# Two attentions in one kernel: Pool's tables, tile 1's low parts and the fourth group's fetches in another order at the start

## The chip, the cores and the metric

One core of a Trainium2 chip. The metric is the time on the device of one execution, in microseconds (us). Five engines work side by side, each in the order of its own queue: TensorE (PE; its weight loads are shown as PEld), VectorE (DVE), ScalarE (ACT), GpSimd (POOL, here Pool) and SyncE (SP), which does nothing here but issue DMAs. An instruction waits until what it needs is done, and everything behind it in its queue waits with it. A DMA that an engine issues goes through the same queue; the transfer then runs by itself and reports when it has landed.

## The reference

`x` is 2048 x 576. Two attentions of 32 heads with 18 features each run over it, and a gate per row mixes them. A has keys and values of its own for each head, B one key and one value for all heads; B's queries and keys are larger, so that its softmax needs true row maxima.

```python
x = A_x                                      # [1, 2048, 576]
g = _sigmoid((x * gate_w).sum(-1, keepdims=True))
# a: q, k, v = split(x @ wqkv), 32 heads of 18
#    o = softmax(q k^T * 18**-0.5) v, then o @ wo
a = _A_ref(x, A_wqkv, A_wo)
# b: q = x @ wq (32 heads), k = x @ wk and v = x @ wv shared by all heads
#    o = softmax(q k^T * 18**-0.5) v, then o @ wo
b = _B_ref(x, B_wq, B_wk, B_wv, B_wo)
return g * a + (1 - g) * b
```

## The kernel before, in words

All float32 work is done in pairs: a number is split into a high part (`h`, rounded to the format that TensorE multiplies fast) and a low part (`l`, the rest), and a product is made of h*h, l*h and h*l. The 64 heads ("units" u, 32 of B and then 32 of A) run one after the other: scores of keys times queries (L752), exponentials on ACT (L760), sums with the values (L767); for each of them the row maxima are taken ahead, 22 key steps early, on VectorE (L707, L716).

**The start.** Before the first scores, `x` is loaded in chunks of 256 columns (c = 0 to 7) into staging tiles (`xs`, `xsh`) and split: `high_x` on ACT, `low_x` on VectorE (L404), and `last_x` (L408), a subtraction on half the partitions, on VectorE or Pool by the chunk. `project` multiplies it with the weights of tile 0 (which holds B's key, the gate, B's value and the first queries) and tile 1, 512 columns at a time. The four stretches of 512 columns are called the first to the fourth group. Each of tile 0 leaves its bank through `leave_first`: `high` on ACT (L283), `low` on VectorE (L287), stores to the DRAM tensor `kq_d` by SP, a copy `pst` on ACT. For odd groups the differences of keys (`pd`, `pdhl`) are stored too, to `kd_d` or `ke_d`. Tile 1 leaves through `leave`, and its store is kept in the list `store`.

Keys and queries then come back from DRAM, three rows per feature: `first_back` (keys' differences `kdb`, the first group of `ksb`, query columns 0 to 1023 of `qs[0]`), `rows_back` (query columns 1024 to 1535 and 1536 to 2047, the third group of `ksb`, and `keb`, the differences of the third and fourth group), `keys_back` (queries of units 1 and 2, the rest of `ksb`, rows of ones). All of these are issued by SP, in that order. `load_w(2, ...)`, the deferred stores of `REST_ROWS` and `store` and the rows of ones are issued by Pool (L472 to L477). Two copies of one number on Pool, `seen` (L471, L474), make Pool wait for a landing first: the first for `qs[0]`, the second for `keb`.

**The lead stage** (`lead_steps`, L1162 to L1166) follows an order written out as a string. A and B are halves of a product of the projection of tiles 1 and 2 ("units" of `lead_units`: each leaves its two banks through ACT into `lst` and `pst2`, two buffers each, and is added, cast, subtracted and stored by Pool). x and y make a row maximum by way of differences: x multiplies queries by `kdb` or `keb` (the columns of the second half of a pair of groups minus those of the first), ACT takes the positive part into `xd` (L1130, four buffers); y multiplies the same queries by `ksb`, and one VectorE instruction (L1136) adds the two and takes the maximum into the table `mx` (its line names `junk` and `mx`). x comes one pair ahead of y: "x1, x2 y1, x3 y2, ...". A runs on one half of TensorE's rows beside B on the other, and x beside y. Seven banks of PSUM go round between A, B, x and y. The products are numbered in this text by their x: 1 to 16 multiply the 16 column steps of `qs[0]` (128 columns each) by `kdb`, 17 to 32 the same steps by `keb`, 33 on belong to `qs[1]`.

The tables `mx` (five, set to -3e38) and `ms` (two, set to 0) and a rounded copy of the identity, `ident_r`, are made by Pool (L499 to L505), behind all of the above in its queue. `mx` must be set before the first maximum writes into it.

Of the kernel before, what the change touches and what calls it, by code (L numbers as in the profile page):

```python
# [8 lines left out]
F32 = mybir.dt.float32  # L9
# [3 lines left out]
OP = mybir.AluOpType  # L13
# [4 lines left out]
S = 2048  # L18
# [138 lines left out]
def gated_mix_kernel(ctx: ExitStack, tc: tile.TileContext, xT, wall, wv, wo, out):  # L157
    nc = tc.nc
    P = 128

    def dma(o, i, eng=None):
        o, i = (x.bitcast(F32) if x.dtype == F32R else x for x in (o, i))
        return (eng or nc.sync).dma_start(o, i)  # L163
# [22 lines left out]
    ident = fixed.tile([P, P], F32, name="ident")  # L186
    make_identity(nc, ident)
    ident_r = fixed.tile([P, P], F32R, name="ident_r")
    qs = [fixed.tile([P, S], F32R, name=f"qs{i}") for i in range(3)]
# [20 lines left out]
    def in_turn(which):  # L210
        return bank_tile(clk.turn(which))
# [52 lines left out]
    def project(mt, c, w, parts=1):  # L264


        fp = in_turn("g")
        g = 512 // parts
        for i in range(parts):
            products(fp, w, c * 512, g * i, g)  # L270
        return fp

    def products(fp, w, x0, p0, g, n0=0, n1=len(PROJ)):

        for n, (a, b, k, kr) in list(enumerate(PROJ))[n0:n1]:
            nc.tensor.matmul(fp[:, p0:p0 + g], w[a][:kr, k, :], X[b][:kr, k, x0 + p0:x0 + p0 + g],
                             start=(n == 0), stop=(n == len(PROJ) - 1))
# [11 lines left out]
    def leave(mt, c, fp, hl=None):  # L289
        hl = hl or high(fp)  # L290
        low(fp, hl)
        return lambda: dma(qk_d[:, mt * P:(mt + 1) * P, c * 512:(c + 1) * 512].rearrange("a p f -> p a f"), hl, nc.gpsimd)

    def leave_first(c, fp):
        cs = slice(c * 512, (c + 1) * 512)
        hl = high(fp)
        to, q = kq_d[54:216, cs].rearrange("(p a) f -> p a f", a=3), hl[QR]
        tk = kq_d[0:54, cs].rearrange("(p a) f -> p a f", a=3)
        if c % 2:
            d = stp.tile([P, 512], F32, name="pd", bufs=1)  # L300
            dhl = stp.tile([P, 2, 512], F32R, name="pdhl", bufs=1)
            nc.vector.tensor_tensor(d[KR], fp[KR], KD[c - 1][KR], op=OP.subtract)
            nc.scalar.activation(dhl[KR, 0, :], d[KR], AF.Copy)
        low(fp, hl)
        dma(to[:, 1:3], q)
        dma(to[:, 0], q[:, 0])
        if c % 2:
            nc.vector.tensor_tensor(dhl[KR, 1, :], d[KR], dhl[KR, 0, :].bitcast(F32), op=OP.subtract)
            td = kd_d[KR] if c == 1 else ke_d
            dma(td[:, 0:2, :], dhl[KR])  # L310
            dma(td[:, 2, :], dhl[KR, 0])
        else:
            dma(tk[:, 0:2], hl[KR])
            dma(tk[:, 2], hl[KR, 0])
        yield
        st = KD[c] = stp.tile([P, 512], F32, name="pst", bufs=4)
        nc.scalar.activation(st, fp, AF.Copy)

        def rest():
            if c % 2:  # L320
                dma(tk[:, 0:2], hl[KR], nc.gpsimd)
                dma(tk[:, 2], hl[KR, 0], nc.gpsimd)
            dma(z_d[cs], st[ROW_G:ROW_G + 1, :], nc.gpsimd)
            dma(qk_d[:, REST, cs].rearrange("a p f -> p a f"), hl[REST], nc.gpsimd)
        REST_ROWS.append(rest)
# [8 lines left out]
    def run(gen):  # L334
        for _ in gen:
            pass
# [5 lines left out]
    def back2(t, i, x0, x1):  # L342
        for b in (SB, MB):
            back(t, i, b, x0, x1)
# [4 lines left out]
        back2(qs[0], 1, 0, 1024)  # L349

    def rows_back():
        back2(qs[0], 1, 1024, 1536)
        back2(qs[0], 1, 1536, S)
        back(ksb, 0, SB, 1024, 1536)
        dma(keb[MB:MB + 54, :], ke_d.rearrange("p a f -> (p a) f"))

    def keys_back():
        back2(qs[1], 2, 0, S)
# [10 lines left out]
    with tc.tile_pool(name="xs", bufs=1, side="right") as xsp:  # L369
        XS = []  # L370

        def load_x(c, rest=None, main=None):
            half = c < 2
            XS.append(xsp.tile([P, NKT, 256 if half else 512], F32, name="xsh" if half else "xs", bufs=2 if half else 3))
            load5(XS[c], xT[:, 256 * c:256 * c + 256] if half else xT[:, 512 * (c - 1):512 * c], rest, main)

        def main_w(st):

            w = {y: wpool.tile([P, NKT, P], F32R, name=f"w{y}", bufs=3) for y in "hl"}
            nc.scalar.activation(w["h"][:, 0:4], st[:, 0:4], AF.Copy)  # L380
            nc.vector.tensor_tensor(w["l"][:, 0:4], st[:, 0:4], w["h"][:, 0:4].bitcast(F32), op=OP.subtract)
            return w

        def last_w(st, w):
            nc.scalar.activation(w["h"][:, 4], st[:, 4], AF.Copy)
            nc.vector.tensor_tensor(w["l"][:, 4], st[:, 4], w["h"][:, 4].bitcast(F32), op=OP.subtract)

        def chunk_of(c):
            return XS[c // 2 + 1][:, :, 256 * (c % 2):256 * (c % 2) + 256] if c > 1 else XS[c]

        def high_x(c):
            nc.scalar.activation(X["h"][:, :, c * 256:(c + 1) * 256], chunk_of(c), AF.Copy)

        def rest_x(c):
            low_x(c, chunk_of(c))
            last_x(c, chunk_of(c))

        def split_x(c):
            high_x(c)
            rest_x(c)  # L400

        def low_x(c, xs):
            cs = slice(c * 256, (c + 1) * 256)
            nc.vector.tensor_tensor(X["l"][:, :, cs], xs[:, 0:4], X["h"][:, 0:4, cs].bitcast(F32), op=OP.subtract)  # L404

        def last_x(c, xs):
            xh = X["h"][64:128, 4, c * 256:(c + 1) * 256]
            (nc.gpsimd if c in (2, 4, 5, 6) else nc.vector).tensor_tensor(xh, xs[64:128, 4], xh.bitcast(F32), op=OP.subtract)  # L408

        W = [load_w(0, nc.scalar)]  # L410
        load_x(0)
        W.append(load_w(1, nc.gpsimd))
        load_x(1, nc.gpsimd)
        nc.scalar.activation(ones, ones, AF.Copy)

        warm = in_turn("m")

        def idle(n):
            for i in range(n):
                nc.tensor.matmul(warm[:, 0:304], ident, vb.rearrange("p k d -> p (k d)"), start=True, stop=True)  # L420

        idle(6)
        for c in range(2, 5):
            load_x(c)

        x0, xh = XS[0], X["h"][:, :, 0:256]
        ST = [W.pop(0) for _ in range(2)]
        WP = [main_w(ST[0])]
        nc.scalar.activation(xh[:, 0:2], x0[:, 0:2], AF.Copy)
        nc.vector.tensor_copy(xh[:, 2:4], x0[:, 2:4])  # L430
        low_x(0, x0)
        last_w(ST[0], WP[0])
        nc.scalar.activation(xh[:, 4], x0[:, 4], AF.Copy)
        last_x(0, x0)
        WP.append(prep_w(ST[1]))
        split_x(1)

        F = [in_turn("g") for _ in range(2)]
        for x in (0, 256):
            for mt in range(2):  # L440
                products(F[mt], WP[mt], 0, x, 256)
        idle(2)
        rows = leave_first(0, F[0])
        next(rows)
        split_x(2)
        split_x(3)
        run(rows)
        REST_ROWS.pop()()
        F0 = project(0, 1, WP[0], 2)
        hl = high(F[1])  # L450
        high_x(4)
        rows = leave_first(1, F0)
        next(rows)
        first_back()
        run(rows)
        store = [leave(1, 0, F[1], hl)]
        rest_x(4)
        split_x(5)
        F1 = project(1, 1, WP[1])
        split_x(6)  # L460
        split_x(7)
        F0 = project(0, 2, WP[0], 2)
        store.append(leave(1, 1, F1))
        run(leave_first(2, F0))
        F0 = project(0, 3, WP[0], 2)
        run(leave_first(3, F0))

    xdp = ph1.enter_context(tc.tile_pool(name="xdp", bufs=1, side="right"))
    keb = xdp.tile([P, 512], F32R, name="keb")
    seen = xdp.tile([P, 2], F32, name="seen")  # L470
    nc.gpsimd.tensor_copy(seen[MB:MB + 1, 0:1], qs[0][MB:MB + 1, 0:1].bitcast(F32))  # L471
    W.append(load_w(2, nc.gpsimd, nc.gpsimd))  # L472
    rows_back()
# [8 lines left out]
    def gates():  # L482
# [8 lines left out]
        yield  # L491
        for i in range(2):
            dma(gu_d[H * i:H * i + H, :], g_d[i:i + 1, :].to_broadcast([H, S]))

    lead = ctx.enter_context(tc.tile_pool(name="lead", bufs=2, side="left"))

    nc.gpsimd.tensor_copy(ident_r, ident)  # L499
    mxs = [lead.tile([P, 16, 4], F32, name=f"mx{i}", bufs=1) for i in range(5)]  # L500
    for t in mxs:
        nc.gpsimd.memset(t, -3e38)
    ms = [lead.tile([P, 32], F32, name=f"m{i}", bufs=1) for i in range(2)]
    for t in ms:
        nc.gpsimd.memset(t, 0.0)  # L505


    L = {("kd", 0): kdb}

# [797 lines left out]
```

## Time and profile before

| | before |
|---|---|
| median of 3 timed runs | 2661.48 us (2660.05 to 2661.74) |
| the profiled execution's own time | 2658.0 us |
| its span, first to last instruction | 2656.2 us |
| granted TensorE clock, mean | 0.995 |
| time from 120 us to 2600 us in which TensorE isn't busy | 0.07 us |

A row of the timeline reads: start and length in us, engine, line of the kernel, operation, what is written <- what is read, shapes, count, and in brackets the idle time of the engine just ahead of it with what ended it. A row of the windows view: the stretch in us, its length, the busy time of an engine (and its instructions), the granted TensorE clock, the DMA engines' share and GB/s. The chain of waits goes back from the last instruction to whatever released each step; its rows have start, length and what. A row of the tile view: line, engine, operation, tile, count: shortest/median/longest in ns, first and last start, shape. Start times count from the first instruction. Of a DMA the timeline shows the issue (on SPq or Pool); "to landing" is the time from there until its data have arrived.

### The profile page before, as it was taken

The page shows a single profiled execution, that of the slowest core. Times are in us where ns is not written, and L with a number is a line of the kernel's source. Part 1 is how long each engine was busy: PE and PEld are TensorE (multiplying, and loading weights), DVE is VectorE, ACT ScalarE, POOL GpSimd, SP SyncE. Part 2 cuts the span into 40 slices and gives each one's busy share as a digit, 9 for nine tenths or more (in the row PEclk, how much of TensorE's full clock was granted, in tenths as well). Part 3 has the DMA queues.
Part 4 walks back from the last instruction along what each step waited for, and adds up shares of the span by engine and source line. Part 5 has one row for each costly group of instructions (what it writes and reads, how often), then busy time and mean ns, then how long its engine had stood idle before and what let it go on. Part 6 is the DMA issues. An engine that isn't in the chain of part 4 may idle for free.

```text
span 2656.2 us, 67494 instructions
## 1 busy us (share of the span) xinstructions
PE 2625.2 (99%) x25423; PEld 1416.7 (53%) x25423; DVE 2393.4 (90%) x4573; ACT 2450.6 (92%) x4864; POOL 951.8 (36%) x1202
## 2 busy tenths in 40 slices
PE   6999999999999999999999999999999999999999
PEld 5545455555554545555454554544555555545665
DVE  4899999899999999999999999999999998999883
ACT  4899999999999999999999999999999999999887
POOL 3434423311035445553555446444541020012213
PEclk8999999999999999999999999999999999999999
DMA  7323213222133324333444345434443433224322
GB/s 210 111 79 93 83 60 93 79 71 63 45 111 110 97 86 118 109 100 89 133 151 137 116 123 155 142 119 137 137 130 96 115 97 92 78 79 124 113 59 92
DMA packets 186035, 280.81 MB, mean 106 GB/s; under 512 B 59947, under 2 KB 147211, under 8 KB 174265
## 3 DMA queue, kind: packets, MB, share of 16 engines
q1 hardware_dynamic: 169309, 222.82, 29.3%
q0 software_dynamic: 15520, 52.30, 5.4%
q8 instruction: 200, 3.28, 0.5%
q10 hardware_dynamic: 880, 1.39, 0.1%
q14 instruction: 126, 1.03, 0.1%
HBM read 200.74 MB, written 66.90 MB: 101 GB/s over the span
## 4 chain that ended last, share of the span: by engine, by line
PE 97%; DMA 1%; POOL 1%; DVE 0%; issue 0%; ACT 0%; SPq 0%; ACTq 0%; DVEq 0%; POOLq 0%
PE acc L767 38%; PE bank L707 28%; PE bank L752 18%; PE bank L975 11%; PE acc L779 1%; PE bank L955 1%; PE bank L1126 0%; DMA xs<-xT 0%; DMA kq<-phl 0%; DMA xsh<-xT 0%; POOL xh L408 0%; POOL oacc L948 0%; SPq L163 0%; DMA keb<-ke 0%; DVE mx L716 0%
## 5 line engine op out<-in xcount | busy, mean ns | idle before, releaser
L760 ACT ACTIVATE pt<-bank 128x512 f32<-128x512 f32 x4096 | 2151.3, 615 | 132.3 <-PE bank L752 67.9
L716 DVE TENSOR_REDUCE mx<-bank 128x1 f32<-128x512 f32 x3002 | 1888.3, 685 | 130.0 <-PE bank L752 61.9
L752 PE MATMUL bank<-qs,ksb 56*128 56x512 f32 x2688 | 914.8, 425 | 1.5 <-DVE mx L713 1.5
L707 PE MATMUL bank<-ksb,qs 54*128 54x512 f32 x2270 | 816.9, 427 | 0.0
L767 PE MATMUL acc<-pt,vb 128*19 128x256 f32 (+3 forms) x6096 | 553.6, 459 | 0.0
L707 PEld LDWEIGHTS bank<-ksb,qs 54*128 54x128 f32 x2270 | 386.4, 185 | 294.7 <-ACT pt L760 163.0
L767 PE MATMUL acc<-pt,vg 128*19 128x512 f32 (+3 forms) x5952 | 531.6, 455 | 0.0
L752 PEld LDWEIGHTS bank<-qs,ksb 56*128 56x128 f32 x2688 | 443.5, 185 | 162.5 <-DVE mx L716 67.0
L752 PE MATMUL bank<-qs,ksa 56*128 56x512 f32 x1408 | 467.9, 425 | 0.1
L707 PE MATMUL bank<-ksa,qs 54*128 54x512 f32 x1232 | 441.5, 425 | 0.0
L713 DVE CUSTOM_DVE_ANT_0 junk<-bank,xb 128x512 bf16<-128x512 f32 x500 | 343.0, 686 | 34.4 <-PE bank L752 28.9
L710 ACT ACTIVATE xb<-bank 128x512 f32<-128x512 f32 x500 | 292.6, 605 | 18.0 <-PE bank L752 9.5
L707 PEld LDWEIGHTS bank<-ksa,qs 54*128 54x128 f32 x1232 | 209.8, 184 | 142.3 <-ACT pt L760 81.0
L752 PEld LDWEIGHTS bank<-qs,ksa 56*128 56x128 f32 x1408 | 225.8, 184 | 84.2 <-DVE mx L716 33.7
L239 POOL CAST rhl<-rst 128x292 fp32r<-128x292 f32 (+2 forms) x95 | 40.0, 421 | 606.6 <-issue 375.3
L767 PEld LDWEIGHTS acc<-pt,vb 128*19 128x19 f32 x6096 | 122.9, 97 | 213.1 <-issue 182.7
L767 PEld LDWEIGHTS acc<-pt,vg 128*19 128x19 f32 x5952 | 121.6, 97 | 211.9 <-issue 185.6
L239 POOL CAST mh<-mt 128x32 fp32r<-128x32 f32 x62 | 13.0, 210 | 561.4 <-DVE mt L725 453.2
L975 PE MATMUL bank<-xr,wrh 64*128 64x292 f32 (+1 forms) x1386 | 205.0, 300 | 0.0
L975 PEld LDWEIGHTS bank<-xr,wrh 64*128 64x128 f32 x1386 | 170.4, 186 | 3.4
L707 PE MATMUL bank<-kdb,qs 54*128 54x512 f32 x372 | 161.3, 434 | 0.0
L570 POOL TENSOR_TENSOR xr<-xst,xr 128x876 fp32r<-128x876 f32 (+1 forms) x77 | 159.3, 2069 | 0.0
(174 smaller groups left out, 2446.1 us busy)
## 6 DMA issues: line engine op xcount, KB each, us to landing
qs<-qk SPq DMA_DIRECT2D x366, 144.0 KB
xst<-xT SPq DMA_DIRECT2D x66, 438.0 KB
qk<-rhl POOLq DMA_DIRECT2D x66, 292.0 KB, 4.5
ksa<-qk SPq DMA_DIRECT2D x132, 144.0 KB
xst<-xT SPq DMA_DIRECT2D x66, 146.0 KB
xst<-xT SPq DMA_DIRECT2D x132, 73.0 KB
ksb<-qk SPq DMA_DIRECT2D x60, 144.0 KB
onh<-oh POOLq DMA_DIRECT2D x32, 256.0 KB, 3.6
```

The costliest lines, as they stand in the source:

```text
L239: eng_h.tensor_copy(h, src)
L570: nc.gpsimd.tensor_tensor(x[:, 5:8, 0:n], t0, x[:, 0:3, 0:n].bitcast(F32), op=OP.subtract)
L707: nc.tensor.matmul(pm, qs[u % 3][b:b + 54, i * P:(i + 1) * P], k, start=True, stop=True)
L710: nc.scalar.activation(MX["x", u, i], pm, AF.Relu)
L713: nc.vector.tensor_tensor_reduce(junk, pm, MX.pop(("x", u, i)), 1.0, -3e38, op0=OP.add, op1=OP.max, accum_out=MX[u][:, i, c:c + 1])
L716: nc.vector.tensor_reduce(MX[u][:, i, c:c + 1], pm, axis=AX.X, op=OP.max)
L752: nc.tensor.matmul(ps, kst(u)[b:b + 56, i * P:(i + 1) * P], qs[u % 3][b:b + 56, c * 512:(c + 1) * 512], start=True, stop=True)
L760: nc.scalar.activation(pt, ps, AF.Exp, scale=SCALE)
L767: nc.tensor.matmul(acc[32 * j:32 * j + 19, a:b], v_of(u, i), PT[u, i, j][:, a:b], start=(i == 0), stop=(i == 15), skip_group_check=True)
L779: nc.tensor.matmul(acc[32 * j:32 * j + 19, 256 * half + a:256 * half + b], v_of(NU - 1, i), pt[:, x + a:x + b], start=(i == 0), stop=(i == ...
L955: nc.tensor.matmul(fp[:, 0:u.n], x, y, start=(n == 0), stop=(n == len(u.ops) - 1))
L975: nc.tensor.matmul(u.fp[op][:, 0:u.n], x[b:b + 64], y[b:b + 64], start=(n == 0), stop=(n == last))
```

## The change

Four things are put in another order; no instruction's work is altered. (1) `ident_r`, `mx` and `ms` are made ahead of the first `seen`. (2) `last_x` of chunks 5 and 6 goes from Pool to VectorE. (3) The first `leave` of tile 1 comes behind the last split, and the second one behind `leave_first(2, ...)`. (4) The third group's queries are fetched right behind the third group's stores, and the fourth group's queries behind `ksb` and `keb`.

```diff
     def rows_back():
-        back2(qs[0], 1, 1024, 1536)
-        back2(qs[0], 1, 1536, S)
         back(ksb, 0, SB, 1024, 1536)
         dma(keb[MB:MB + 54, :], ke_d.rearrange("p a f -> (p a) f"))
+        back2(qs[0], 1, 1536, S)
...
-            (nc.gpsimd if c in (2, 4, 5, 6) else nc.vector).tensor_tensor(xh, xs[64:128, 4], xh.bitcast(F32), op=OP.subtract)
+            (nc.gpsimd if c in (2, 4) else nc.vector).tensor_tensor(xh, xs[64:128, 4], xh.bitcast(F32), op=OP.subtract)
...
-        store = [leave(1, 0, F[1], hl)]
         rest_x(4)
         split_x(5)
         F1 = project(1, 1, WP[1])
         split_x(6)
         split_x(7)
+        store = [leave(1, 0, F[1], hl)]
         F0 = project(0, 2, WP[0], 2)
+        run(leave_first(2, F0))
         store.append(leave(1, 1, F1))
-        run(leave_first(2, F0))
+        back2(qs[0], 1, 1024, 1536)
         F0 = project(0, 3, WP[0], 2)
         run(leave_first(3, F0))
...
     seen = xdp.tile([P, 2], F32, name="seen")
+    lead = ctx.enter_context(tc.tile_pool(name="lead", bufs=2, side="left"))
+    nc.gpsimd.tensor_copy(ident_r, ident)
+    mxs = [lead.tile([P, 16, 4], F32, name=f"mx{i}", bufs=1) for i in range(5)]
+    for t in mxs:
+        nc.gpsimd.memset(t, -3e38)
+    ms = [lead.tile([P, 32], F32, name=f"m{i}", bufs=1) for i in range(2)]
+    for t in ms:
+        nc.gpsimd.memset(t, 0.0)
     nc.gpsimd.tensor_copy(seen[MB:MB + 1, 0:1], qs[0][MB:MB + 1, 0:1].bitcast(F32))
     W.append(load_w(2, nc.gpsimd, nc.gpsimd))
     rows_back()
...
-    lead = ctx.enter_context(tc.tile_pool(name="lead", bufs=2, side="left"))
-    nc.gpsimd.tensor_copy(ident_r, ident)
-    mxs = [lead.tile([P, 16, 4], F32, name=f"mx{i}", bufs=1) for i in range(5)]
-    for t in mxs:
-        nc.gpsimd.memset(t, -3e38)
-    ms = [lead.tile([P, 32], F32, name=f"m{i}", bufs=1) for i in range(2)]
-    for t in ms:
-        nc.gpsimd.memset(t, 0.0)
```

Pool's queue at the end of its deferred stores, before the change (`phl` are the split rows on their way to `qk_d`):

```order
L163 DMA qk<-phl 24x2x512
L163 DMA qk<-phl 128x2x512 x2
L163 DMA ones_r<-ones 128x32
L499 CAST ident_r<-ident 128x128
L502 MEMSET mx_458 128x64
L502 MEMSET mx_459 128x64
L502 MEMSET mx_460 128x64
```

and Pool's queue of the changed kernel from its second `last_x` (L407 there) to its second wait for a landing:

```order
L407 TENSOR_TENSOR xh<-xs,xh 64x256
L472 CAST ident_r<-ident 128x128
L475 MEMSET mx_421 128x64
L475 MEMSET mx_422 128x64
L475 MEMSET mx_423 128x64
L475 MEMSET mx_424 128x64
L475 MEMSET mx_425 128x64
L478 MEMSET m_431 128x32
L478 MEMSET m_432 128x32
L479 COPY seen<-qs_90 1x1
L163 DMA wst<-wall 128x512
```

The cast and the seven memsets have moved from behind both `seen` and the deferred stores to ahead of the first `seen`, and two `last_x` have left the queue.

SP's queue, from the third group's last key stores to the queries of unit 1 (`qs_90` is `qs[0]`, `qs_91` is `qs[1]`; the first `kq<-phl` rows with 54 rows below the plus sign are the fourth group's):

```order
 L163 DMA kq<-phl 18x2x512
 L163 DMA kq<-phl 18x512
+L163 DMA qs_90<-kq 64x512 x2
 L163 DMA kq<-phl 54x2x512
 L163 DMA kq<-phl 54x512
 L163 DMA ke<-pdhl 18x1024
 L163 DMA ke<-pdhl 18x512
-L163 DMA qs_90<-kq 64x512 x4
 L163 DMA ksb<-kq 64x512
 L163 DMA keb<-ke 54x512
+L163 DMA qs_90<-kq 64x512 x2
 L163 DMA qs_91<-kq 64x2048 x2
```

Two of the four query fetches stand ahead of the fourth group's stores now, the other two behind `keb`.

VectorE's queue at the splits of chunks 4 to 7, before (`bank_172` is tile 1's first bank, `bank_304` its second, `bank_325` the third group's):

```order
L308 TENSOR_TENSOR pdhl<-pd,pdhl 18x512
L287 TENSOR_TENSOR phl<-bank_172,phl 128x512
L404 TENSOR_TENSOR xl<-xs,xh 128x4x256 x4
L408 TENSOR_TENSOR xh<-xs,xh 64x256
L287 TENSOR_TENSOR phl<-bank_304,phl 128x512
L287 TENSOR_TENSOR phl<-bank_325,phl 128x512
```

and in the changed kernel (`bank_303` is tile 1's second bank there):

```order
L308 TENSOR_TENSOR pdhl<-pd,pdhl 18x512
L403 TENSOR_TENSOR xl<-xs,xh 128x4x256 x2
L407 TENSOR_TENSOR xh<-xs,xh 64x256
L403 TENSOR_TENSOR xl<-xs,xh 128x4x256
L407 TENSOR_TENSOR xh<-xs,xh 64x256
L403 TENSOR_TENSOR xl<-xs,xh 128x4x256
L407 TENSOR_TENSOR xh<-xs,xh 64x256
L287 TENSOR_TENSOR phl<-bank_172,phl 128x512
L287 TENSOR_TENSOR phl<-bank_325,phl 128x512
L287 TENSOR_TENSOR phl<-bank_303,phl 128x512
```

Two `last_x` stand between the low parts, tile 1's first low part has moved behind all of them, and its second one behind the third group's.

## The prediction

> **What bounds the kernel now.** The page comes first: one number on it says where not to look.
>
> ```profile
> span 2656.2 us, 67494 instructions
> PE 2625.2 (99%) x25423; PEld 1416.7 (53%) x25423; DVE 2393.4 (90%) x4573; ACT 2450.6 (92%) x4864; POOL 951.8 (36%) x1202
> ```
>
> TensorE is busy in all but 31.0 us (2656.2 - 2625.2). The windows view then finds where these lie (stretch, PE busy, granted clock, DMA):
>
> ```profile
> 37.00:55.00 18.00, 1.33 (x12) 0.62 0.75 202
> 120.00:2600.00 2480.00, 2479.93 (x24226) 1.00 0.35 103
> ```
>
> Over half of it, 18.00 - 1.33 = 16.67 us, lies between 37 and 55 us, and from 120 us on nothing is missing. The change touches only code that runs before 60 us, so what it does to that hole is what it does to the kernel: behind it TensorE works without a pause and carries any shift to the end. The timeline shows what the hole waits for (start, length, engine, line, operation; idle before it in brackets).
>
> ```profile
> 34.53 0.47 PE L1126 MATMUL bank<-kdb,qs 54*128 54x512 f32 x1 [0.25 <-DMA qs<-kq]
> 36.36 2.06 ACT L1130 ACTIVATE xd<-bank 128x512 f32<-128x512 f32 x4
> 45.37 0.18 POOL L474 COPY seen<-keb 1x1 f32<-1x1 f32 x1 [8.51 <-DMA keb<-ke]
> 45.59 1.16 POOL L163 DMA_DIRECT2D kq<-phl  x2
> 53.13 0.56 POOL L163 DMA_DIRECT2D ones_r<-ones  x1
> 53.73 0.29 POOL L499 CAST ident_r<-ident 128x128 fp32r<-128x128 f32 x1
> 53.97 0.49 POOL L502 MEMSET mx<- 128x64 f32 x5
> 54.15 0.69 DVE L1136 CUSTOM_DVE_ANT_0 junk<-bank,xd 128x512 bf16<-128x512 f32 x1 [17.53 <-POOL mx L502]
> 54.90 0.79 PE L1126 MATMUL bank<-kdb,qs 54*128 54x512 f32 x1 [16.67 <-DVE mx L1136]
> ```
>
> The lead stage (score products, their maxima on VectorE) can start at 34.53, when the queries have landed. Its first maximum writes into the table `mx`. Pool fills that table only at 53.97, since the memset stands in its queue behind `seen`, which waits for `keb` to land (45.37), and behind thirteen DMA issues (45.59 to 53.69). VectorE waits 17.53 us, the seven banks fill up, TensorE stops.
>
> **Part 1: the tables ahead of Pool's waits.** Now the cast and seven memsets stand behind Pool's last `last_x`, and the first memset waits only for the x staging space (its last reader is `last_x(7)` on VectorE, near 30 us). They take 0.85 us there (53.73 to 54.58 before), beside nothing that needs Pool until `seen` at 34.5. So VectorE no longer waits for `mx`; what is late next is the next input of the products. They go in the order of the code: 1 to 8 need query columns 0 to 1023, 9 to 12 the third group (1024 to 1535), 13 to 16 the fourth, 17 on `keb` with the third group of `ksb`. Where product 13 stands, and how fast they go, is in the tile view of `kdb` for two windows (count, first and last start):
>
> ```profile
> L1126 PE MATMUL bank<-kdb,qs x13: 387/397/789, 34.5 to 61.8; 54*128 54x512 f32 x13
> L1126 PE MATMUL bank<-kdb,qs x8: 387/481/789, 34.5 to 58.4; 54*128 54x512 f32 x8
> ```
>
> Product 5 runs at 54.9, 8 at 58.4, 13 at 61.75 (a row below has the exact start). From 8 to 13 the order string has 13 pairs of half-array products, 3.35 us, 0.26 us each. From 1 to 13 it has 31: 8.1 us, so unhindered product 13 is due at 34.5 + 8.1 = **42.6**. VectorE isn't later than what follows: ACT's first `xd` began at 36.36, right after the fourth group's copies, which won't be later; with its maximum by 37.0 and eleven more at 0.69 or less, the twelfth starts by 44.6. Product 9 is due after 21 pairs, at 40.0.
>
> **Part 2: the split.** `last_x` of chunks 5 and 6 moves from Pool to VectorE, and the low part of tile 1 goes behind the splits.
>
> ```profile
> 29.89 0.92 POOL L408 TENSOR_TENSOR xh<-xs,xh 64x256 fp32r<-64x256 f32 x1
> 20.02 0.42 DVE L408 TENSOR_TENSOR xh<-xs,xh 64x256 fp32r<-64x256 f32 x1
> 24.14 0.67 DVE L287 TENSOR_TENSOR phl<-bank,phl 128x512 fp32r<-128x512 f32 x1
> 24.74 4.61 DVE L404 TENSOR_TENSOR xl<-xs,xh 128x1024 fp32r<-128x1024 f32 x4
> 31.16 0.69 DVE L287 TENSOR_TENSOR phl<-bank,phl 128x512 fp32r<-128x512 f32 x1 [0.22 <-ACT phl L283]
> 25.30 4.64 POOL xh L408
> ```
>
> On Pool one of these took 4.64 us (last row, from the chain) beside VectorE's four low parts; on VectorE it takes 0.42. New order: four low parts from 24.14 (4.61), three `last_x` (1.26) to 30.0, tile 1's low part to 30.65, then the third group's low part to 31.3 instead of 31.85: **0.55 us earlier**. TensorE is done with the projections earlier, too, but that is worth nothing by itself: product 1 still waits for the queries at 34.5, whose fetch is not moved. It pays only through the stores.
>
> **Part 3: the queue of SP.** The third group's two fetches move ahead of the fourth group's four stores, the fourth group's behind `ksb` and `keb`.
>
> ```profile
> 31.88 4.69 SPq L163 DMA_DIRECT2D kq<-phl  x6
> 36.66 1.99 SPq L163 DMA_DIRECT2D ke<-pdhl  x2
> 38.75 2.37 SPq L163 DMA_DIRECT2D qs<-kq  x4
> 41.16 0.60 SPq L163 DMA_DIRECT2D ksb<-kq  x1
> 41.94 0.36 SPq L163 DMA_DIRECT2D keb<-ke  x1
> 42.34 1.08 SPq L163 DMA_DIRECT2D qs<-kq  x2
> DMA to landing us min/median/max: 2.0/3.1/4.4
> 41.94 3.37 DMA keb<-ke
> 36.22 3.76 DMA kq<-phl
> 61.75 0.39 PE L1126 MATMUL bank<-kdb,qs 54*128 54x512 f32 x1
> ```
>
> The third group's stores go out at 31.3 and 31.6 and land by 35.4 (the 3.76 of the chain); the new wait for them holds everything behind it in SP's queue. Two fetches (1.09) to 36.5: the third group lands by 39.4 to 40.0, just as product 9 is due, cost 0. The fourth group's two stores go out 36.5 to 37.2 (35.9 before: **0.6 later**, which eats the 0.55), `ke` 1.99 to 39.2, `ksb` to 39.8. `keb` waits for `ke`: second issue 38.6 + 3.1 = 41.7, bounds 40.6 and 43.0. Then the fourth group: its second half, which product 13 reads, is issued near 42.4 and lands 3.1 later. I take **45.4**, a little below the 45.5 this gives, since `keb` left no later than 3.3 us after the last `ke` before. With 2.0 or 4.4 at these last two landings it is 43.5 or 48.3. So product 13, due at 42.6, waits for 2.8 us: a second, smaller hole. Against 61.75 it comes 61.75 - 45.4 = **16.35 us earlier** (13.5 to 18.2). The next inputs have cover: `keb` lands 3.4 after 41.7, at 45.1, ahead of product 17; the 56-row products, the first to need all of `ksb` and its ones, come at 89.9 - 16 = 74, while the ones go out at 60.7 by Pool's queue, which moves with `keb` by 0.3:
>
> ```profile
> 60.71 0.53 SPq L163 DMA_DIRECT2D ksb<-ones_r  x2
> 89.87 1.09 PE L752 MATMUL bank<-qs,ksb 56*128 56x512 f32 x4
> ```
>
> Without that cover each late us would cost one.
>
> **Two deductions.** The clock, and Pool's backlog.
>
> ```profile
> 54.82:58.23 3.41, 3.33 (x16) 0.50 0.95 279
> 34.34:37.75 3.41, 2.65 (x18) 1.00 0.49 135
> 116.26:119.67 3.41, 1.92 (x14) 1.00 0.41 98
> 119.67:123.09 3.42, 3.42 (x30) 0.50 0.21 74
> 60.46 1.29 POOL L1113 TENSOR_TENSOR lst<-lst,pst 128x512 f32<-128x512 f32 x1 [5.88 <-ACT pst L991]
> 64.09 0.73 POOL L163 DMA_DIRECT2D qk<-phl  x1 [0.30 <-POOL phl L241]
> 72.99 0.59 ACT L985 ACTIVATE lst<-bank 128x512 f32<-128x512 f32 x1
> ```
>
> After the hole the clock was 0.50 until 58.23: products 5 to 8 (8 pairs) took 3.5 us where 0.26 each makes 2.1, a loss of 1.4 that 16.35 already has on the before side. The new hole can bring it again behind product 13: a stretch with 1.92 us of work in 3.41 was followed by half clock, one with 2.65 was not. 2.8 us of rest leaves 0.6 to 2 us of work in a stretch, by where its edges fall. Nothing to 1.4; I take **0.7**. [...]
>
> Pool: its thirteen issues still follow `keb`, ending near 53.4, and only then does it take up the first unit (add, cast, subtract: from 60.46 to 64.09 - 0.30, 3.35 us), to 56.75. Its buffers, two of them, are wanted by the third unit at 72.99 - 16.35 = 56.6. Stall 0 to 0.7, taken **0.3**.
>
> **The sum.** 16.35 - 0.7 - 0.3 = 15.35. The profiled execution took 2658.0 us (span 2656.2 and 1.8 around it): 2642.65. The three timed runs have their median 3.5 us above that, at 2661.48, and the same saving there gives **2646.1 us**. Worst terms: 13.5 - 1.4 - 0.7 = 11.4, 2650.1; best 18.2, 2643.3.
>
> **Rivals.** *No second hole*: the fourth group lands by 42.6, the gain is 61.75 - 42.6 = 19.15: 2642.3 (2643.3 at 43.5). For it speaks the 2.0 us minimum, against it the 3.37 and 3.76 of the chain, and three transfers that follow each other. 0.08. *A wider hole*: SP's new wait for the third group's stores comes late, `ke` and `keb` follow, and Pool, whose issues follow `keb`, stalls ACT at the third unit as well. With every latency at 4.4 and both deductions full it is 2650, and each us more in `keb` counts nearly twice: 2648.5 to 2653. 0.18. *The change doesn't free VectorE*: the memsets run early, but the first maximum waits for something else that ends near 54, 2661. The brackets name only `mx` for the 17.53, and bank and `xd` of four products were ready at 38.4. 0.03. *Slower*: Pool's thirteen issues now run beside a busy VectorE, not an idle one. If each were held as `last_x` was (4.64 in place of 0.92 or less, +3.7), the queue would end 48 us later, near 101; the third unit's buffers would come free at 104.8 in place of 56.75, and the kernel would lose 48 - 16 = 32: 2693. From 1.3 us more per issue on (13 of them against 16.35) the change loses. Against it: the issue at 64.09, in the middle of VectorE's maxima, took 0.73, those in the hole 0.56 and 0.58. 0.04. [...]
>
> **How the numbers follow.** Forecast 2646.1, own range 2644 to 2648.5, chance 0.67; with the wider hole 0.18, the early landing 0.08, no effect 0.03, slower 0.04. The range 2642.5 to 2651.5 takes in the bounds of the sum (2643.3, 2650.1) and most of the wider hole. A measurement here tells 0.2%, 5.3 us, from no change: faster is under 2656.2, chance 0.92; same 0.04; slower 0.04.
>
> **What would show it.** Right: memsets of `mx` near 30 us; the first maximum near 36; the third group's stores near 31.3; `keb` seen by Pool near 45; one TensorE hole of about 3 us that ends at 45 to 46 on a landing of `qs`; the 56-row products first at 73 to 75. Wrong: a wait of VectorE for Pool or of ACT for `lst` over 1 us, Pool's issues over 0.9 us each, a hole at product 9 (third group late) or 17 (`keb` late), or a shift at 90 us that is gone by 130.

## The result, and the profile after

| | before | after |
|---|---|---|
| median | 2661.06 us (2660.05 to 2661.74, 4 runs) | 2643.97 us (2641.16 to 2645.47, 4 runs) |
| ratio, with its 95% interval | | 0.9935 (0.9918 to 0.9952) |
| the profiled execution's own time | 2658.0 us | 2644.58 us |
| both kernels once more, beside each other on one chip (9 and 5 runs) | 2658.49 us | 2644.85 us, ratio 0.9948 (0.9934 to 0.9961) |

The kernel is faster: 17.1 us by the medians, 13.4 by the two profiled executions, 13.6 by the repetition. The forecast was 2646.1, in a range of 2642.5 to 2651.5; of the narrower range given with it, 2644 to 2648.5, the median misses the lower end by 0.03 us, and the repetition lies in it.

The page of the kernel after shows no change that the eye would catch; TensorE now lacks 16.5 us of work (2642.8 - 2626.3), where it lacked 31.0.

```profile
span 2642.8 us, 67497 instructions
PE 2626.3 (99%) x25423; PEld 1420.7 (54%) x25423; DVE 2394.1 (91%) x4575; ACT 2451.4 (93%) x4864; POOL 948.2 (36%) x1200
```

The windows view of the kernel after (stretch, length, PE busy, granted clock, DMA share, GB/s) shows where: of the 16.67 us of hole between 37 and 55 us, 4.37 are left (18.00 - 13.63). The clock, 0.62 there before, is 0.78; the two stretches behind have 0.92.

```profile
31.00:37.00 6.00, 3.67 (x21) 0.78 0.61 192
37.00:55.00 18.00, 13.63 (x90) 0.78 0.63 185
55.00:75.00 20.00, 20.00 (x152) 0.92 0.67 217
75.00:120.00 45.00, 43.44 (x367) 0.92 0.39 114
120.00:2600.00 2480.00, 2479.92 (x24246) 1.00 0.34 102
```

The timeline of the kernel after, engine by engine (Pool, VectorE, SP, TensorE, ACT). The tables are set near 30 us, the first maximum starts at 35.33, and TensorE has two waits for `qs` (2.33 and 2.84 us) in place of one for `mx`. The first comes at product 1, the second at product 13.

```profile
29.84 0.49 POOL L475 MEMSET mx<- 128x64 f32 x5 [7.66 <-DVE xh L407]
43.15 0.18 POOL L482 COPY seen<-keb 1x1 f32<-1x1 f32 x1 [7.50 <-DMA keb<-ke]
44.53 0.53 POOL L163 DMA_DIRECT2D z_d<-pst  x1
53.45 0.56 POOL L163 DMA_DIRECT2D ones_r<-ones  x1
35.33 0.69 DVE L1131 CUSTOM_DVE_ANT_0 junk<-bank,xd 128x512 bf16<-128x512 f32 x1 [0.48 <-PE bank L970]
31.08 2.44 SPq L163 DMA_DIRECT2D kq<-phl  x4
34.87 1.10 SPq L163 DMA_DIRECT2D qs<-kq  x2
36.08 0.82 SPq L163 DMA_DIRECT2D kq<-phl  x2
36.94 1.95 SPq L163 DMA_DIRECT2D ke<-pdhl  x2
40.71 0.26 SPq L163 DMA_DIRECT2D keb<-ke  x1
41.07 3.22 SPq L163 DMA_DIRECT2D qs<-kq  x4
33.53 0.46 PE L1121 MATMUL bank<-kdb,qs 54*128 54x512 f32 x1 [2.33 <-DMA qs<-kq]
46.27 0.47 PE L1121 MATMUL bank<-kdb,qs 54*128 54x512 f32 x1 [2.84 <-DMA qs<-kq]
47.88 1.80 PE L330 MATMUL bank<-ident,pst 18*128 18x18 f32 x16
60.87 0.59 ACT L980 ACTIVATE lst<-bank 128x512 f32<-128x512 f32 x1
```

(The lines of the lead stage have numbers smaller by 5 than before: L1121 is the product x or y, L970 a half of a unit, L980 the copy into `lst`.)

Far more than the forecast allowed for is what the clock did behind that wait. The windows view again, cut along the 3.41 us stretches in which the clock is granted:

```profile
30.98:34.39 3.41, 1.08 (x10) 1.00 0.66 207
34.39:37.80 3.41, 3.41 (x19) 0.50 0.54 172
41.22:44.63 3.41, 2.22 (x17) 1.00 0.62 153
44.63:48.04 3.41, 1.76 (x15) 1.00 0.88 240
48.04:51.46 3.42, 3.42 (x24) 0.50 0.57 158
51.46:54.87 3.41, 2.04 (x10) 0.50 0.60 199
54.87:58.28 3.41, 3.41 (x18) 0.50 1.02 287
58.28:61.70 3.42, 3.42 (x29) 1.00 0.70 246
```

The stretch with the second hole (1.76 us of work) is followed by half clock, and this stays for three stretches, 10.2 us. The sixteen small transposes behind product 15 (L330) show it: 1.80 us in place of 1.17 before. What it costs is read in the tile view of `keb`: its first sixteen products, 17 to 32, start at 67.7 to 77.5 us before (first row) and at 53.6 to 65.4 after (second row).

```profile
L1126 PE MATMUL bank<-keb,qs x16: 386/392/491, 67.7 to 77.5; 54*128 54x512 f32 x16
```

```profile
L1121 PE MATMUL bank<-keb,qs x16: 388/398/625, 53.6 to 65.4; 54*128 54x512 f32 x16
```

So the shift against before is 15.5 us at product 13 (61.75 - 46.27), 14.1 at product 17, 12.1 at product 32. Of this 1.3 us come back by the end (13.4): 0.8 us between the first exponential and the twentieth (90.6 to 102.9 us before, 78.5 to 90.1 here), a span in which the clock was halved for 6.8 us before and for 3.4 here, the rest spread over the program. The prediction had the shift carried to the end unchanged, so this 1.3 us is a gain that it did not foresee.

### The profile page after: what moved, and what is told of

The parts are those of the page before. It is cut to its first block, busy times and chain, and to the rows that moved or that the text cites. A ratio compares the mean times of both kernels' runs of the same rounds, so it can differ in the third digit from the quotient of the medians.

```text
span 2642.8 us, 67497 instructions
## 1 busy us (share of the span) xinstructions
PE 2626.3 (99%) x25423; PEld 1420.7 (54%) x25423; DVE 2394.1 (91%) x4575; ACT 2451.4 (93%) x4864; POOL 948.2 (36%) x1200
## 3 DMA queue, kind: packets, MB, share of 16 engines
q8 instruction: 200, 3.28, 0.5%
q10 hardware_dynamic: 880, 1.39, 0.1%
## 4 chain that ended last, share of the span: by engine, by line
PE 97%; DMA 2%; DVE 0%; SPq 0%; ACT 0%; issue 0%; POOL 0%; ACTq 0%
PE acc L762 38%; PE bank L702 29%; PE bank L747 18%; PE bank L970 11%; PE bank L1121 1%; DMA xs<-xT 0%; PE bank L950 0%; DMA qs<-kq 0%; SPq L163 0%; PE acc L774 0%; DMA wst<-wall 0%; DMA R<-r_d 0%; POOL oacc L943 0%; DVE mx L711 0%; DMA kd<-pdhl 0%
## 5 line engine op out<-in xcount | busy, mean ns | idle before, releaser
L970 PE MATMUL bank<-xr,wrh 64*128 64x292 f32 (+1 forms) x1386 | 205.2, 300 | 0.0
L970 PEld LDWEIGHTS bank<-xr,wrh 64*128 64x128 f32 x1386 | 170.4, 186 | 3.4
```

Of the source, the lines that this page charges most:

```text
L970: nc.tensor.matmul(u.fp[op][:, 0:u.n], x[b:b + 64], y[b:b + 64], start=(n == 0), stop=(n == last))
```

## The experiments

All times below are medians, and each ratio is to the kernel before on the same chip: 2659.48 us for e1 to e4, 2655.15 for e5 to e8, 2658.49 for f1 to f4. Since the chips differ by up to 4.3 us, times are compared within one of these three groups, and across them only by the ratios.

**e1: part 1 alone.** In the kernel before, the block that makes the tables is moved, nothing else.

```diff
+    nc.gpsimd.tensor_copy(ident_r, ident)
+    mxs = [lead.tile([P, 16, 4], F32, name=f"mx{i}", bufs=1) for i in range(5)]
...
     nc.gpsimd.tensor_copy(seen[MB:MB + 1, 0:1], qs[0][MB:MB + 1, 0:1].bitcast(F32))
...
-    nc.gpsimd.tensor_copy(ident_r, ident)
...
```

> The kernel before with part 1 alone: tables and rounded identity made ahead of Pool's waits, split and queue of SP as before. My theory (the maxima are freed, and from then on the landing of the queries sets the time): the wait of VectorE for mx of 17.5 us is gone, the first maximum comes near 36, and the hole of TensorE moves to product 9, since the third group lands as late as before (42 to 43 us) while product 9 is due near 40; product 13 then follows with no hole of its own, near 45.5. Time 2645 to 2649. Rival 'the order of SP's queue carries a part of the gain': product 13 only after 48, time 2650 to 2655. Rival 'mx was not what held VectorE': 2661.

Measured: 2642.91 us, ratio 0.9937 (0.9924 to 0.9949), a gain of 16.6 us; I had expected 2645 to 2649. TensorE's timeline has the hole at product 9, for the third group, as expected, and no wait at product 13 (45.5).

```profile
43.07 0.47 PE L1121 MATMUL bank<-kdb,qs 54*128 54x512 f32 x1 [1.98 <-DMA qs<-kq]
```

Part 1 alone gives the whole gain. In its profile no half clock came between 8 and 79 us.

**e2: all but part 1.** The kernel after with the block back behind Pool's issues.

> The kernel after with part 1 undone: split and queue of SP as after, tables behind Pool's thirteen issues. My theory: VectorE waits for mx until 51.5 to 54 again (keb lands some 2 us earlier than before, so Pool may begin its issues 2 us earlier), TensorE stands still for 15 to 17 us, time 2659 to 2661, a gain of 0 to 2 us. Rival 'earlier projections and fetches are worth something by themselves': 2650 to 2657.

Measured: 2660.4 us, ratio 1.0001 (0.9992 to 1.001). Parts 2 and 3 without part 1 give nothing; the waits view has VectorE waiting for `mx` again, 21.4 us (to 56.55, later than the 51.5 to 54 that I expected):

```profile
DVE junk L1132 <- POOL mx L499: 21.4, 1, 21.4
PE bank L1122 <- DVE mx L1132: 19.0, 1, 19.0
```

**e3: part 2 undone.**

```diff
-            (nc.gpsimd if c in (2, 4) else nc.vector).tensor_tensor(xh, ...
+            (nc.gpsimd if c in (2, 4, 5, 6) else nc.vector).tensor_tensor(xh, ...
...
+        store = [leave(1, 0, F[1], hl)]
         rest_x(4)
...
-        store = [leave(1, 0, F[1], hl)]
         F0 = project(0, 2, WP[0], 2)
+        store.append(leave(1, 1, F1))
         run(leave_first(2, F0))
-        store.append(leave(1, 1, F1))
```

> The kernel after with part 2 undone: last_x of chunks 5 and 6 on Pool again, tile 1's low parts at their old places. My theory: the third group's low part comes 0.5 us later, and so do its stores, its fetch and the fourth group's fetch; product 13 is 0.3 to 1 us later than the 46.27 of the profile after, time 2644 to 2645.5 (the kernel after: 2643.97). Rival 'the split is why product 1 came at 33.5 in place of 34.5': product 1 back at 34.5 here. By my theory that was the fetch landing sooner by chance, and product 1 lies anywhere from 33.5 to 34.6. Rival 'the split is worth nothing': time 2643.5 to 2644.

Measured: 2644.92 us, ratio 0.9942 (0.9929 to 0.9954). That lies between the two measurements of the kernel after (0.9935 and 0.9948): what part 2 is worth can't be measured here. Product 13 came at 44.87, not later but 1.4 us earlier than in the profile after, and product 1 at 33.15 without the new split. So the rival that the split brought product 1 forward falls.

**e4 and f2: part 3 undone.** The kernel after with the order of SP's queue as before: both fetches together, behind the fourth group's stores and `ke`, ahead of `ksb` and `keb`. It was run twice, the second time beside the kernel after.

```diff
     def rows_back():
+        back2(qs[0], 1, 1024, 1536)
+        back2(qs[0], 1, 1536, S)
         back(ksb, 0, SB, 1024, 1536)
         dma(keb[MB:MB + 54, :], ke_d.rearrange("p a f -> (p a) f"))
-        back2(qs[0], 1, 1536, S)
...
-        back2(qs[0], 1, 1024, 1536)
         F0 = project(0, 3, WP[0], 2)
```

> The kernel after with part 3 undone: third and fourth group's queries fetched as before, behind the fourth group's stores and ke, ahead of ksb and keb. My theory: this order only puts the second hole at another place; it lies at product 9 (the third group lands at 41.5 to 42.8, due near 39.5), 2 to 3 us long, and product 13 needs no wait; product 13 starts at 45 to 46.5, as with the new order, time 2642.5 to 2647. Rival 'the new queue order is what keeps the hole short': hole over 4 us, 2648 or more.

> The kernel after once more, unchanged, on the same chip as the three others of this call. It tells how much of the differences between kernels is the chip and the run: ten profiles so far have product 1 at 31.7 to 35.1 us whatever the edit. Expected: product 1 in that range, a second hole of 2 to 3 us at product 13, half clock behind it where the 3.41 us stretch with the hole holds under 1.8 us of work, gain over before 14 to 17 us.

> The kernel of e4 (part 3 undone) once more, beside f1. Theory 'part 3 costs time, since its hole at product 13 is the longer one and brings the half clock': 1 to 2.5 us faster than f1, and no half clock between 40 and 60 us. Rival 'part 3 makes no difference, e4 was a better chip or a better draw': within 0.7 us of f1.

| | runs | median | ratio to before |
|---|---|---|---|
| e4, part 3 undone | 2639.61 to 2642.94 | 2641.92 | 0.9930 (0.9916 to 0.9944) |
| f2, the same | 2639.35 to 2642.42 | 2639.58 | 0.9934 (0.9921 to 0.9946) |
| f1, the kernel after | 2641.66 to 2646.10 | 2644.85 | 0.9948 (0.9934 to 0.9961) |

Beside each other the kernel without part 3 is 5.3 us faster than the kernel after; over all runs of both (ten and nine) the medians are 2640.77 and 2644.58, 3.8 us apart. The ratios' intervals overlap, so the size is uncertain, but part 3 gains nothing, and most likely loses 2 to 5 us. Both results lie below what I had expected: e4 under its 2642.5, f2 more than 2.5 us faster than f1. The timelines of SP, TensorE and ACT in e4 tell how:

```profile
32.95 3.73 SPq L163 DMA_DIRECT2D kq<-phl  x6
39.29 2.43 SPq L163 DMA_DIRECT2D qs<-kq  x4
42.55 0.36 SPq L163 DMA_DIRECT2D keb<-ke  x1
42.99 0.47 PE L1121 MATMUL bank<-kdb,qs 54*128 54x512 f32 x1 [2.05 <-DMA qs<-kq]
47.18 1.17 PE L330 MATMUL bank<-ident,pst 18*128 18x18 f32 x16
58.27 0.60 ACT L980 ACTIVATE lst<-bank 128x512 f32<-128x512 f32 x1 [1.50 <-POOL phl L241]
```

The fourth group's two stores go out with the third group's (x6 in 3.73 us), all four fetches follow in one run, and product 13 starts at 45.43 although the third group's stores left 1.9 us later than in the kernel after (32.95 against 31.08). Measured from the start of these stores, product 13 comes after 12.5 to 13.4 us in the four profiles with the old order where no half clock held it (e1, e4, f2, e7), and after 14.0 to 15.7 in four with the new one (after, f1, e3, e6). The new order costs about 2 us there, on the mean of 12.8 against 14.9 (f4, with the old order and half clock in this span, needed 13.5).

Then the clock: the old order's hole at product 9 is 1.98 us in e1, 2.05 in e4 and 0.79 in f2 (there it ends on ACT's copy into `lst`, not on a landing), the new order's at 13 is 2.84 in after, 2.98 in f1 and 2.18 in e3. In f1 the stretch with the hole held 1.00 us of work, in e4 1.92, and only the first was followed by half clock. The windows view at that place, first of f1, then of e4:

```profile
44.02:47.43 3.41, 1.00 (x8) 1.00 0.74 190
47.43:50.84 3.41, 3.41 (x24) 0.50 0.96 229
```

```profile
41.50:44.91 3.41, 1.92 (x15) 1.00 0.71 234
44.91:48.33 3.42, 3.42 (x37) 1.00 1.01 230
```

From product 13 to 17 it takes 5.95 us in e4 (5.96 before), 7.37 in after, 7.91 in f1. The old order isn't safe from it: in f4 the hole of 2.12 us at product 9 left 1.30 us of work in its stretch, and half clock followed. In these rows half clock follows the stretches with 1.00, 1.30 and (in after) 1.76 us of work and not the one with 1.92, which in before did have it behind it (116.26 to 119.67); so it also matters how the hole falls on the stretches.

At product 32 the old order was 2.6 us ahead in e4 (62.77, after 65.38) and 2.7 in f2 (62.74, f1 65.47). By the end of the spans the lead was 1.7 us (2641.1, 2642.8) and 6.5 us (2637.8, 2644.3), with half clock behind the first 56-row products for 10.2 us in e4, 6.8 in after, 10.2 in f1 and none in f2. So in both pairs some 2.6 us are won up to product 32, and what happens behind it, for reasons not known, spreads the rest. The timed runs agree with the clock as the larger part: their mean granted clock is 0.995 to 0.998 in the nine of the kernel after (mean 0.9961), and 0.997 to 0.999 in the ten without part 3 (mean 0.9979). The difference, 0.0018 of 2642 us, makes 4.8 us, which is an estimate; the medians are 3.8 us apart.

**e6 and f3: fillers in the second hole.** The kernel after, with products that nothing needs ahead of product 13, eight and then fourteen (768 columns each, 0.35 us), as additional work.

```diff
-               "yABxyABABxyABxyvABABxy..."
+               "yABffffffffxyABABxyABxyvABABxy..."
```

> The kernel after with eight filler products (768 columns each, into a bank that nothing reads before it is written anew) ahead of product 13, to keep TensorE busy in the second hole. Theory 'the hole brings the half clock': no half clock between 45 and 58 us, the transposes after product 15 take 1.1 in place of 1.8 us, product 17 comes at 52 to 52.6 in place of 53.64, time 2641.5 to 2643 (part of it given back to Pool's backlog). Rival 'the half clock comes from the first hole or by itself, at fixed times': half clock there as before, 2643.5 to 2645. Rival 'the fillers hold product 13 up': it starts later than 47.

> The kernel after with fourteen filler products ahead of product 13 in place of the eight of e6, whose fillers (0.35 us each) ran out 1.86 us before the queries landed. Theory 'a stretch with too little work brings the half clock': the fillers leave less than 1 us of rest, no half clock between 43 and 60 us, product 17 follows product 13 in 5.9 to 6.1 us (7.4 in after, 8.7 in e6), time 1 to 2 us under f1 unless the fillers hold product 13 up. Rival 'half clock comes whatever TensorE does there': half clock after 43 us as in after and e6.

e6, 2642.47 us, ratio 0.9952 (0.994 to 0.9965), decides nothing. Half clock came all the same, where the theory had none, but the hole had not been filled: product 9 was early (37.95), the fillers were used up by 43.83, TensorE rested 1.86 us more, and the stretch held 1.83 us of work. f3, 2643.13 us, ratio 0.9943 (0.993 to 0.9955), decides it. In its windows the stretches around product 13 are full and the clock stays; half clock comes only behind the next pause, the 1.56 us in which TensorE waits for ACT's cast of tile 2's weights (second fence, from its timeline).

```profile
41.00:44.42 3.42, 3.28 (x24) 1.00 0.31 93
44.42:47.83 3.41, 3.41 (x23) 1.00 0.75 203
47.83:51.24 3.41, 3.41 (x36) 1.00 0.94 210
51.24:54.66 3.42, 1.85 (x16) 1.00 0.36 128
54.66:58.07 3.41, 3.41 (x18) 0.50 0.94 260
```

```profile
54.13 0.50 PE L970 MATMUL bank<-xh,wh 64*128 64x512 f32 x2 [1.56 <-ACT wh L249]
```

From product 13 to 17 it took 6.33 us (expected 5.9 to 6.1), 1.6 less than in f1. But the fillers, from 44.15 on, ran up to product 13 (48.13) and past it, TensorE rested nowhere ahead of it, and product 17 was no earlier than in f1 (54.46 and 54.33). The time, 1.7 us under f1's, has an interval that overlaps f1's: the mechanism is shown, the gain isn't.

**e7: a third buffer for lst.** e4 with `lst` in three buffers (`junk2` in two, for room).

```diff
-            st = xdp.tile([P, 512], F32, name="lst", bufs=2)
+            st = xdp.tile([P, 512], F32, name="lst", bufs=3)
...
```

> The kernel of e4 (part 3 undone) with three buffers in place of two for lst (and two in place of three for junk2, to make room). Theory 'Pool's backlog costs what ACT waits at the third unit': that wait, 1.50 us in e4, is gone, the shift at product 32 is 16 us in place of 14.7, time 2640.3 to 2641.0 (e4: 2641.92). Rival 'the wait only moves on to the fourth unit or to Pool's stores': a wait of ACT for Pool of over 0.7 at a later unit, 2641.5 to 2642.3.

Measured: 2640.54 us, ratio 0.9946 (0.9932 to 0.9959). ACT's wait for Pool is gone, and TensorE loses nothing between products 17 and 32: 9.8 us as in before, where e4 took 11.4 (tile view of `keb`, first of e4, then of e7).

```profile
L1121 PE MATMUL bank<-keb,qs x16: 388/392/496, 51.4 to 62.8; 54*128 54x512 f32 x16
```

```profile
L1121 PE MATMUL bank<-keb,qs x16: 388/393/496, 49.7 to 59.5; 54*128 54x512 f32 x16
```

So Pool's backlog does cost what ACT waits at the third unit: 1.50 us of waiting in e4, 1.6 us of TensorE's time. The total doesn't show it: the ratio, on another chip, is no better than e4's.

**e5 and e8: the fourth group's stores first.** The kernel after with the third group's fetch behind the fourth group's two stores, and the fourth group's fetch ahead of `ksb` and `keb`; e8 has e7's buffers too.

```diff
         dma(to[:, 0], q[:, 0])
+        if c == 3:
+            back2(qs[0], 1, 1024, 1536)
...
     def rows_back():
+        back2(qs[0], 1, 1536, S)
...
```

> The kernel after with SP's queue in a third order: the fourth group's two stores go ahead of the third group's fetches (whose landing they no longer wait for), and the fourth group's fetches stand ahead of ksb and keb. No landing should be late now: third group at 39.5 to 40.5, fourth at 41.5 to 43, product 13 at 42.5 to 43.5, 2 us or more ahead of the 45.43 of e4. Two theories. 'The landings alone set the time': 2639 to 2640, 2 to 3 us less than e4 (2641.92). 'Pool's backlog is the next limit': its thirteen issues still follow keb (44.5 to 45.5), the third unit finds lst taken until 57.5 to 58, the wait of ACT for Pool grows from 1.5 in e4 to about 3.5 us and gives it all back, time 2641 to 2642.5. I hold the second.

> Both edits of e5 and e7: SP's third order and three lst buffers. If landings and Pool's backlog are the two limits: product 13 at 42.5 to 43.5, no wait of ACT for Pool over 1 us at the third unit, time 2638 to 2639.5, the lowest so far. If a third limit takes over (the fourth unit's buffers, ACT itself, the weights of tile 2): within 1 us of e7.

Measured: 2641.04 us, ratio 0.9946 (0.9933 to 0.9958), and 2640.9 us, ratio 0.9945 (0.9933 to 0.9958). The holes are nearly gone: in e5 TensorE waits 0.43 us at product 9 and not at all at 13 (41.89), in e8 0.43 at 13. No gain over e4 or e7 can be measured. In e5 ACT waited 1.39 us for Pool, not 3.5, since `keb` was seen at 42.55, earlier than I took; in e8 that wait is gone. So neither of e5's theories foretold its numbers: its time lies in the range of the second, but the wait that was to bring it there did not. e8 is 0.4 us from e7, as its theory of a third limit has it; what that limit is was not looked for.

**f4: tile 2's weights split one unit earlier,** on top of e7.

```diff
-            if mt == len(WP):
+            if (mt, c) == (1, 3):
```

> The kernel of e7 (part 3 undone, three lst buffers) with the split of tile 2's weights taken ahead by one unit: ACT's cast wh (0.74 us) stood behind the copy of the second unit, and TensorE waited 1.56 us for it in e7 (1.37 in after). Theory: that wait goes, 1 to 1.5 us less than e7 relative to before, 3 to 5 us less than f1. Rival: VectorE's maxima are the next limit (the 0.74 us wait for mx at 64.4 in e7 grows) and give most of it back, within 0.5 us of e7's gain of 14.6.

Measured: 2641.69 us, ratio 0.9937 (0.9925 to 0.995), 3.2 us under f1 and 2.1 over f2. Against before it gains 16.8 us where e7 gained 14.6, but on another chip and with intervals that overlap. The wait of 1.56 us is gone (from product 13 to 17 it takes 4.49 us), but three pieces of half clock fell elsewhere in its profile (43.2 to 46.6, 77.3 to 84.2, 104.6 to 108.0). It is no better than f2. The best version on record is the kernel with part 3 undone: faster than before by 17.6 us (e4) and 18.9 (f2), and most likely, but not beyond the intervals, faster than the kernel after.

## Why the prediction was right, point by point

**Part 1, VectorE is freed: right, and all of the gain.** Memsets at 29.84 (near 30), first maximum at 35.33 (near 36). e1 and e2 show that this part alone has it.

**Part 2, 0.55 us on the third group's stores, worth nothing by itself: not told apart.** The stores left at 31.08, and e3 without the part has them at 30.85. Such starts move by more than the term between executions: product 1 came at 33.53 and 33.50 in the kernel after, at 35.13 and 33.45 in e4 and f2, at 31.70 in e5, at 34.53 before. So its 1.0 us in the profile after can't be put down to the change; I had held its start fixed at 34.5.

**Part 3, the third group at no cost: right.** Product 9 ran without a wait (40.05; due 40.0). That the time fits is luck: product 1 came 1.0 us early, and the 21 pairs from there took 6.5 us where I had reckoned 5.5.

**Part 3, the fourth group at 45.4: right in kind, 0.9 us short.** The hole is where it was put, 2.84 us (2.8) on a landing of `qs`; product 13 started at 46.27. The length fits by luck, since both ends of the hole came late: it began at 43.4, not 42.6, and ended 0.9 us behind its forecast. `keb` left earlier than I had it (40.71 against 41.7), so did the fetch (41.62 for its second half, against 42.4), but it landed after 4.5 us, beyond the 4.4 of my longest bound. The chain of waits after:

```profile
41.62 4.52 DMA qs<-kq
```

What I left out is the other side: the old order behind an early table. Its hole is at product 9, its product 13 about 2 us earlier, counted from the third group's stores. I priced part 3 only as it stands, not against its own removal.

**The clock, 0.7 us (0 to 1.4): the mis-sized term.** From product 13 to 32 the kernel after took 19.1 us where before took 15.7 (65.4 - 46.27 and 77.5 - 61.75), 3.4 us more; f1 19.1 again. I had reckoned with one stretch of half clock of at most 1.4 us; it was three. Why the clock did not come back after the first (48.04 to 51.46), which the profile shows as full, isn't known; the second held only 2.04 us of work, since the pause of 1.37 us at tile 2's weights fell into it, and the clock came back after the third. f3 shows that the hole brings it: with the hole filled (3.41 us of work from 44.42 to 47.83) the clock is 1.00 up to 54.66, the end of the stretch with that pause (1.56 us there).

**Pool's backlog, 0.3 us (0 to 0.7): 0 in the profile after,** as the half clock made the third unit late enough (its copy at 60.87, without a wait). Where no half clock came between product 13 and that copy, it was 1.16 us in e1, 1.5 in e4, 2.32 in f2, and e7 shows that this costs time. (In f2 half clock followed that wait, from 57.36 to 60.77, where I had expected none.) So the two deductions don't add up: the one hides the other.

**The sum.** 15.5 - 3.4 + 1.3 that came back by the end makes 13.4, against 15.35. The 1.3 had no term in the prediction; 0.8 of it falls in the span that had 3.4 us less of half clock than before, for a reason that isn't known, and so is luck. The 17.1 of the first medians and the 13.6 of f1 stand on the two sides of it. The median gain is larger than the profiled one, since the profiled execution of before lay 3.1 us under its median and that of after 0.6 over; so the forecast, made from the profile and carried over to the median, came 2.1 us too high, though its terms were 1.9 us too hopeful. That the two errors have opposite signs is luck; what was right is the mechanism and the size of its largest term. The 56-row products, said to begin at 73 to 75, began at 77.8, by the late landing and the clock.

**The rivals.** The three of no second hole, of VectorE not freed and of a slower kernel are excluded by the profile: Pool's thirteen issues, now beside VectorE's maxima, took 0.51 to 0.75 us each (0.53 and 0.56 in the rows shown above). A wider hole of 2648.5 or more was not seen.

## What to carry to other kernels

When one late instruction holds a whole stage, move that alone first and look at it: here a cast and seven memsets behind a wait for a landing cost 16.6 us, and the rest of the change, made in the same step, hid that one part of it most likely gave some of this back. Price each part of a change against its own removal, not only against the kernel before. And count the TensorE clock as part of a hole: here pauses of 2.84 us (after) and 2.98 us (f1) were followed by half clock, and products 13 to 32 then took 3.4 us more than in before (19.1 against 15.7).

## What the runs showed of the hardware

- The granted clock changed at the edges of stretches of 3.41 us (in after 34.39, 37.80, 48.04 and 58.28 us). Of those at full clock between 24 and 126 us in the fourteen profiles, all 13 that held under 1.7 us of TensorE work were followed by half clock, 11 of the 27 that held 1.76 to 2.26 us, and 1 of the 48 that held 2.26 to 3.3 (it belongs to the next point). None of the 13 was empty of work. Followed by half clock were, for instance, 0.48 us of work (before, 37.75), 1.00 (f1, 44.02), 1.08 (after, 30.98), 1.66 (f2, 53.95), 1.76 (after, 44.63) and 1.85 (f3, 51.24); not followed by it 1.84 (f2, 47.12), 1.92 (e4, 41.50), 2.22 (after, 41.22) and 3.28 (f3, 41.00).
- In 13 of the fourteen profiles half clock also comes at 2.5 to 5.1 us behind the first 56-row products (in before at 92.37, the products from 89.87 on; in after at 82.18, from 77.8 on), for one to three stretches, 12 times straight after a stretch shown as full (busy time counts modelled ends). f2 alone went without, and gained 3 us against e4 there (from product 32 to the fiftieth exponential 43.4 us, against 46.5). What brings it was not tried.
- The start of the lead stage, which waits for landings, varies: product 1 lay between 31.7 and 35.1 us in fourteen profiles, 1.7 us apart in e4 and f2, which are the same kernel, and 0.04 in after and f1. Most of it is there when SP issues the fetch that product 1 reads: its second half left at 30.86 us in e4 and at 29.23 in f2. What makes a fetch take 4.5 us in one place and 3.1 at the median isn't known; that two more fetches followed it closely in the queue need not be the reason, since in e8, where they were further behind, it took 4.36.
- The format of the high parts is multiplied faster than plain float32: in before four products of plain float32 with 304 columns (L420, from 16.02 us) took 1.18 us, four of that format with 256 columns (L276, from 17.69) 0.64, 0.97 and 0.63 ns a column, both at clock 1.00.
